# Attention, then a gated MLP: the last quarter's error function is written to four PSUM banks, the out-projection rotates through the other four

## The chip, the cores and the metric

The kernel runs on one core of one Trainium2 chip. The metric is the device time of one execution in microseconds (us), lower is better. Engines are named as the profile names them: PE (TensorE, matrix products; PEld its weight loads), DVE (VectorE), ACT (ScalarE), POOL (GpSimd), SP (SyncE, which issues DMAs). SBUF is the large on-chip memory, PSUM the small one that PE writes its products to; it has eight banks of 128 x 512 float32.

## The reference

Two stages, the second of which matters here. The first is an attention with a routing mask; its result, 3072 tokens of 512 numbers, is the `x` of an MLP whose gate is an error function of a softplus:

```python
def _moe_ref(x, w_in, w_out):          # x 3072x512, w_in 512x2048, w_out 2048x512
    h = x @ w_in
    sp = np.maximum(h, 0.0) + np.log1p(np.exp(-np.abs(h)))
    g = h * erf(sp)
    return (g @ w_out).astype(np.float32)
```

## The kernel before, in words

**The stages.** The first part of the kernel (up to about 404 us) is the attention. The rest is the MLP over six chunks of 512 tokens. Chunks 0 and 1 are worked one by one: the hidden layer `h` in two lots (`hidden26`, then `hidden`), then the out-projection (`project26`, line 1213, called with no plan). Chunks 2 to 5 go in pairs, with a hidden layer of another form (`hidden49`) and `project26` with a plan; the change leaves their computation as it is.

**The products.** Both layers are computed with fast matrix multiplication: sums and differences of blocks are formed first, fewer block products are made than there are pairs of blocks, and the products are added with signs into the results. The hidden layer of chunks 0 and 1 makes seven products where eight would be needed. The out-projection makes 26 (lists `LEFT` and `RIGHT`, line 70; the loop over `p` at line 1286). One product is four matmuls of 128 x 128 by 128 x 256 in float32, eight records in the trace.

**The gate.** Before the out-projection may read a block of `h`, it is gated: ACT computes the softplus of it into a buffer, then the error function of that in the same place, and DVE multiplies it into `g` (`gate26`, line 850). A call covers a quarter of a chunk's hidden layer, in two pieces `s` of 128 x 1024; each piece gets one softplus, one error function and two multiplications of 128 x 512. The last quarter (lot 1, half 1) is gated inside the out-projection itself (lines 1226 to 1231): softplus ahead of p = 0 and behind it, error functions at p = 1 and 2 (`s` = 1 first), multiplications (1,1), (0,1), (0,0), (1,0) of (s, h) at p = 3, 4, 5 and 6. Its buffer is, in chunk 0, the place of chunk 1's input `x_own` (`x_of[1]`, free until it is loaded at p = 8), and in chunk 1 a buffer `a_s`. At p = 4 and 5 of chunk 0 two multiplications of the quarter before also stand.

**Around the products.** `LEFT_STEPS` says which sums of gated blocks DVE forms behind which `p` (in place, so that such a step may wait until PE has read the old block); the products that use them follow a few `p` later. `AFTER` says how product `p` is read out of its bank: 'c' is a copy by ACT, 'a' an addition by DVE; capital letters go on from SBUF alone. The read-out of `p` is issued behind product `p + 1` (`LAG`). Each engine works in the order in which the program issues, all waits are semaphores. In chunk 0 POOL forms sums of blocks of `w_out` (`FIRST_FORMS`, `LAST_FORMS`, 128 x 512 each), of which the last stand at the beginning of the out-projection.

**The banks.** `bank()` gives the next of eight banks (lines 714 to 722): six of the pool `psb`, which rotates, and the two tiles `turned`. Within the out-projection product `p` takes the next bank at each `p`, so a bank comes round again after eight products.

Of the kernel before, what the change touches and what calls it, by code (L numbers as in the profile page):

```python
# [9 lines left out]
F32 = mybir.dt.float32  # L10
# [4 lines left out]
ALU = mybir.AluOpType  # L15
ACT = mybir.ActivationFunctionType
AX = mybir.AxisListType
PSUM = bass.MemoryType.PSUM

P = 128  # L20
# [15 lines left out]
HT, HK, HF, HM = CT // 2, DM // P // 2, NFT // 2, DM // 2  # L36
# [109 lines left out]
def kernel(  # L146
# [13 lines left out]
    te, ve, ae, ge = (  # L160
        InOrder(tc, e, in_order) for e in (nc.tensor, nc.vector, nc.scalar, nc.gpsimd)
    )

    def pool(name, bufs, **kw):
        return ctx.enter_context(tc.tile_pool(name=name, bufs=bufs, **kw))
# [5 lines left out]
    turned = [ps.tile([P, 512], F32, name=f"turned{i}") for i in range(2)]  # L171
# [100 lines left out]
    for base, pattern, sign, op, fill in (  # L272
# [5 lines left out]
            out=first, in_=first, compare_op=op, fill=fill, base=base, pattern=pattern,  # L278
# [355 lines left out]
    def load_x(n, queue=nc.sync):  # L634
        if n < NCHUNK:
            if n not in x_of:
                x_of[n] = xp.tile([P, DM // P, CT], F32, name="x_own")
            queue.dma_start(
                out=x_of[n], in_=x_dram.rearrange("(k p) t -> p k t", p=P)[:, :, n * CT : (n + 1) * CT]
            )  # L640

    def minus_of(out, a, b, engine=ve):
        engine.tensor_tensor(out=out, in0=a, in1=b, op=ALU.subtract)

    def plus_of(out, a, b, engine=ve):
        engine.tensor_tensor(out=out, in0=a, in1=b, op=ALU.add)
# [19 lines left out]
    def coming(n):  # L666
        return range(n + 1, 2 * n + 2) if n < N49 else range(n + 2, min(n + 4, NCHUNK)) if n % 2 == 0 else ()
# [41 lines left out]
    ORDER = (1, 2, 6, 7, 5, 3, 4)  # L709
    aside_work = []  # L710
    n_banks = [0]
    banks = [None]

    def whole_bank():
        n_banks[0] += 1
        b = banks[n_banks[0] % len(banks)]
        if b is None:
            b = psb.tile([P, 512], F32, name="bank")
        return b

    def bank():
        return whole_bank()[:, 0:HT]
# [68 lines left out]
    def w_block(b):  # L791
        lot, h = KAPPA[b // 2]
        f = h * HF + lot * FG
        return w_out[:, f : f + FG, (b % 2) * HM : (b % 2 + 1) * HM]

    def slot(i):
        if i < 6:
            at = HOME[i]
            return more_out[:, at // 2, (at % 2) * FG : (at % 2 + 1) * FG]
        return w_block((4, 7)[i - 6]) if i < 8 else ring[i - 8]  # L800
# [34 lines left out]
    def load_stream(k, queue=nc.sync):  # L835
        queue.dma_start(out=flat(ring[(k + 2) % RING]), in_=b_dram[k % N_STREAM])

    def left26(n, i):
        if i >= 16:
            return extra[i - 16]  # L840
        lot, h = KAPPA[i % 4]
        t = i // 4
        return g_of[n, t // 2, lot][:, h, :, (t % 2) * P : (t % 2 + 1) * P]

    def left_step(n, x, engine=ve):
        _, o, a, b, sign = LEFT_STEPS[x]
        form = plus_of if sign > 0 else minus_of
        form(left26(n, o), left26(n, a), left26(n, b), engine)

    def gate26(n, lot, half, boxes=None):  # L850
        gs = [g_of[n, s, lot][:, :, 2 * half : 2 * half + 2].rearrange("p h j t -> p h (j t)") for s in range(2)]
        box = []

        def soft(s):
            if not s:
                box.extend(boxes() if boxes else halves_of(actp.tile([P, 2 * FG * HT], F32, name="a_s")))
            ae.activation(out=box[s].rearrange("p (h j) -> p h j", h=2), in_=gs[s], func=ACT.Softplus)

        def erf(s):
            ae.activation(out=box[s], in_=box[s], func=ACT.Erf)  # L860

        def product(s, h):
            c = slice(h * 512, (h + 1) * 512)
            ve.tensor_tensor(out=gs[s][:, h], in0=box[s][:, c], in1=gs[s][:, h], op=ALU.mult)

        halves = [[functools.partial(f, s) for s in range(2)] for f in (soft, erf)]
        return *halves, {(s, h): functools.partial(product, s, h) for s in range(2) for h in range(2)}

    def halves_of(t):
        return [t[:, s * 1024 : (s + 1) * 1024] for s in range(2)]  # L870
# [38 lines left out]
    def load49(i, queue=nc.sync):  # L909
        o, a = w_order[i % len(w_order)]  # L910
        queue.dma_start(out=w49_place(i), in_=a_dram[OUTER.index(o), KEPT_AT[a]])
# [18 lines left out]
    def add49(o, lot, k):  # L930
        return [
            functools.partial(ge.dma_start, out=form49(o)[:, a], in_=part, accum_op=ALU.add)
            for a, part in w49_parts(lot, k)
        ]
# [274 lines left out]
    def fence(after):  # L1209
        t = up.tile([P, HM], F32, name="u")  # L1210
        ge.tensor_tensor(out=t[:, 0:1], in0=after[:, 0:1], in1=after[:, 0:1], op=ALU.add)

    def project26(n, plan=None):
# [4 lines left out]
        def c_at(i):  # L1218
            if i >= 8:
                return temps[i - 8]  # L1220
            t = i // 2
            return osb_of[n, t // 2][:, t % 2, (i % 2) * HM : (i % 2 + 1) * HM]

        if plan is None:
            boxes = None if n else lambda: halves_of(x_of[1].rearrange("p k t -> p (k t)"))
            soft, erf, last = gate26(n, 1, 1, boxes)
            curves = {-1: soft[:1], 0: soft[1:], 1: erf[1:], 2: erf[:1]}
            early = gates_first.pop(n)[1 + 4 * n :]
            gates_at = {
                -1: early[:2], 3: [last[1, 1]], 4: [last[0, 1], *early[2:3]], 5: [last[0, 0], *early[3:]], 6: [last[1, 0]],  # L1230
            }
            gates_before = {}
        else:
            gates_at, (curves, gates_before) = {}, plan
# [3 lines left out]
        banks26 = {}  # L1238
# [45 lines left out]
                    last_forms[p + i] = [piece]  # L1284
        run(f() for f in curves.get(-1, []) + gates_at.get(-1, []) + last_forms[-1])
        for p, r in enumerate(right):
            banks26[p] = m = bank()
            lhs = left26(n, left[p])
            g26 = N_STREAM * q + r - 100
            rhs = ring[(g26 + 2) % RING] if r >= 100 else slot(r) if r >= 0 else w_block(-1 - r)  # L1290
            for f in range(FG):
                te.matmul(m, lhsT=lhs[:, f], rhs=rhs[:, f], start=(f == 0), stop=(f == FG - 1))
            if r >= 100:
                if (g26 + RING) // N_STREAM in (q, q + 1 - q % 2):
                    load_stream(g26 + RING, queue)
            run(f() for f in last_forms.get(p, []) + gates_before.get(p, []))
            for x, step in enumerate(LEFT_STEPS):
                if step[0] == p:
                    left_step(n, x)
            run(f() for f in curves.get(p, ()))  # L1300
            if p < 3:
                if not delayed:
                    evict(p)
            elif p == 3 and delayed:
                for i in range(3):
                    evict(i)
            elif p > 3:
                evict(p - LAG)
                if final and p == len(RIGHT) - 2:
                    plus_of(c_at(2), c_at(2), c_at(8))  # L1310
                    minus_of(c_at(4), c_at(4), c_at(8))
            run(f() for f in gates_at.get(p, ()))
            if p >= len(RIGHT) - 8 and between:
                between.pop(0)()
            if n >= N49 and p in (5, 14) and coming(n):
                load_x(coming(n)[p // 14])
            if p == 14 and n == N49 - 1:
                load_x(n + 2, sy)
            if p == 8 and not n:
                load_x(1, sy)  # L1320
            if n == N49 - 1 and p in range(8, 8 + 2 * W_RING, 2):
                load49(p // 2 - 4, sy)
            if p == 4 and n == N49 - 1:
                fence(c_at(8))
                run(f() for f in add49(3, 0, 1))
# [6 lines left out]
    def run(work):  # L1332
        for _ in work:
            pass
# [137 lines left out]
    for e in range(2):  # L1472
        ae.copy(
            out=ccT[e * D : (e + 1) * D, :, e * C : (e + 1) * C],
            in_=pct[e * D : (e + 1) * D].rearrange("d (r e c) -> d r e c", e=2, c=C)[:, :, e],
# [7 lines left out]
    for r in (0, D):  # L1483
        for half in range(2):
            for e in range(2):
                c = r + half * Q + e * C
                ve.tensor_copy(
                    out=pick[r : r + D, half, e * D : (e + 1) * D].rearrange("p (n c) -> p n c", n=2)[:, :, 1 : C + 1],
                    in_=first[r : r + D, c : c + C].unsqueeze(1).to_broadcast([D, 2, C]),
# [47 lines left out]
    last = divide(u - 1)  # L1537
    attention.close()

    psb = pool("psb", 6, space=PSUM)  # L1540
    gp = pool("gp", 4)
    outp = pool("outp", 2)
    gsp = pool("gsp", 4)
# [2 lines left out]

    def finish_attention():
        run(last)
        banks[:] = [None] * 6 + turned

    take_places(4)
    late_places(2, out_boxes())
# [64 lines left out]
```

## Time and profile before

| | us |
|---|---|
| median of 3 runs | 950.21 (950.09 to 950.82) |
| the profiled execution | 950.18 |
| its span, first to last instruction | 948.4 |
| PE busy in the span | 938.9 (99%) |
| DVE / ACT / POOL busy | 755.8 / 560.2 / 524.3 |
| chunk 0's out-projection, in the span | 454.6 to 501.4 |
| chunk 1's out-projection | 549.7 to 594.6 |

The granted clock of PE is full in every slice of the page. In a row of the timeline stand the start and the length in us, engine, line, operation, output <- inputs by tile names, partitions x elements and type, the number of instructions merged in the row, and in brackets the engine's idle time before it with what ended it. Nearly all instructions have line 137, the helper that issues them, so the names of the tiles tell them apart: `bank` and `turned` are PSUM banks, `g` is the hidden layer, `g_more` holds sums and temporaries, `osb` output blocks, `x_own` and `a_s` (in the multiplications) the buffers of the gate.

### The profile page before, as it was taken

What the parts mean: (1) busy time and instruction counts of PE and PEld (TensorE: products, weight loads), DVE (VectorE), ACT (ScalarE), POOL (GpSimd) and SP (SyncE); (2) the same over time, 40 slices, a digit from 0 to 9 for tenths busy, and PEclk for the clock granted to TensorE, in tenths of its full rate; (3) what the DMA queues carried; (4) which work ended last, traced back from release to release, by engine and by line L of the source; (5) the groups of instructions that cost most, each with busy time, mean ns of one, the idle gap of its engine ahead of it and who ended that gap; (6) DMA issues with size and microseconds to landing.
All of it is one profiled execution on the core that took longest, in us unless ns stands there. A gap on an engine that the chain in (4) does not pass through costs nothing.

```text
span 948.4 us, 20923 instructions
## 1 busy us (share of the span) xinstructions
PE 938.9 (99%) x8151; PEld 691.9 (73%) x8151; DVE 755.8 (80%) x1336; ACT 560.2 (59%) x876; POOL 524.3 (55%) x353
## 2 busy tenths in 40 slices
PE   8999999999999999999999999999999999999998
PEld 3555555555555555588888888888888888888887
DVE  8888888888888888788995778456796974768977
ACT  3788878888888877576323542357825225574341
POOL 1688888888888888999605010676600028770000
PEclk9999999999999999999999999999999999999999
DMA  9454444444444521664659977555645535534443
GB/s 210 92 113 111 113 108 109 111 113 113 113 112 100 119 56 35 226 230 179 212 191 233 206 193 252 161 150 178 196 140 175 156 110 156 177 90 119 150 132 111
DMA packets 183360, 138.74 MB, mean 146 GB/s; under 512 B 132032, under 2 KB 141248, under 8 KB 183232
## 3 DMA queue, kind: packets, MB, share of 16 engines
q1 hardware_dynamic: 176048, 127.83, 47.1%
q0 software_dynamic: 4720, 9.18, 5.5%
q8 instruction: 64, 1.05, 0.5%
q10 hardware_dynamic: 2496, 0.43, 0.2%
q14 instruction: 32, 0.26, 0.1%
HBM read 99.39 MB, written 39.85 MB: 147 GB/s over the span
## 4 chain that ended last, share of the span: by engine, by line
PE 49%; DVE 1%; issue 0%
PE bank L137 39%; PE turned L137 10%; DVE g L137 1%; DVE g_more L137 0%; DVE osb L137 0%; DVE more_out L137 0%; DVE x_own L137 0%
## 5 line engine op out<-in xcount | busy, mean ns | idle before, releaser
L137 POOL TENSOR_TENSOR more_out<-more_out,pr 128x768 f32<-128x768 f32 x128 | 223.8, 1749 | 14.3 <-ACT pr L137 5.7
L137 DVE TENSOR_REDUCE nmx<-wide 128x2 f32<-128x512 f32 (+2 forms) x189 | 180.5, 955 | 51.8 <-PE wide L137 51.1
L137 ACT ACTIVATE pr<-sc 128x768 f32<-128x768 f32 x192 | 148.5, 810 | 65.3 <-PE wide L137 59.3
L137 PE MATMUL turned<-pr,in_v 128*32 128x193 f32 x3072 | 144.8, 330 | 0.0
L137 PEld LDWEIGHTS turned<-pr,in_v 128*32 128x32 f32 x3072 | 91.5, 109 | 51.5 <-issue 26.2
L137 PE MATMUL sc<-qT,kT 64*128 64x384 f32 x528 | 98.8, 488 | 0.0
L137 POOL TENSOR_TENSOR more_out<-pr,pr 128x768 f32<-128x768 f32 x32 | 60.8, 1901 | 41.8 <-ACT pr L137 41.8
L137 POOL TENSOR_TENSOR u<-w_in 128x1 f32<-128x1 f32 x2 | 0.4, 189 | 139.2 <-DVE w_in L137 139.2
L137 DVE TENSOR_TENSOR g<-g 128x512 f32<-128x512 f32 x88 | 62.4, 709 | 16.0 <-PE turned L137 8.5
L137 PE MATMUL bank<-x_own,more_in 128*128 128x256 f32 x276 | 68.1, 379 | 0.0
L137 PE MATMUL bank<-g_more,more_in 128*128 128x256 f32 x288 | 66.5, 380 | 0.0
L137 PE MATMUL wide<-kv,qv 64*128 64x256 bf16 (+2 forms) x378 | 64.0, 328 | 1.4 <-DVE nmx L137 0.9
L137 ACT ACTIVATE x_own<-x_own 128x512 int32<-128x512 uint32 (+2 forms) x62 | 63.0, 1028 | 0.1
L137 PE MATMUL wide<-km,qm 64*128 64x256 bf16 (+3 forms) x378 | 62.6, 327 | 0.0
L137 PEld LDWEIGHTS sc<-qT,kT 64*128 64x128 f32 x528 | 47.3, 187 | 20.6 <-ACT inv L137 3.4
L137 PE MATMUL bank<-g_more,g 128*128 128x256 f32 x256 | 60.6, 380 | 0.7 <-DVE g L137 0.7
L137 PEld LDWEIGHTS bank<-g_more,more_in 128*128 128x128 f32 x288 | 54.6, 190 | 8.2 <-DVE g L137 0.8
L137 PEld LDWEIGHTS bank<-x_own,more_in 128*128 128x128 f32 x276 | 52.4, 190 | 7.1
L137 DVE TENSOR_TENSOR g<-g,bank 128x256 f32<-128x256 f32 (+1 forms) x83 | 41.0, 512 | 20.4 <-PE bank L137 13.6
L137 ACT ACT_TABLE_LOAD x36 | 46.2, 1283 | 16.5 <-DVE g L137 15.9
L137 PEld LDWEIGHTS <-qv 64*128 64x128 bf16 x384 | 23.2, 93 | 42.9 <-issue 26.7
L137 PEld LDWEIGHTS bank<-g_more,g 128*128 128x128 f32 x256 | 48.5, 190 | 7.9 <-issue 1.4
(249 smaller groups left out, 2090.1 us busy)
## 6 DMA issues: line engine op xcount, KB each, us to landing
g_more<-b_dram SPq DMA_DIRECT2D x57, 512.0 KB, 3.7
more_in<-a_dram SPq DMA_DIRECT2D x98, 256.0 KB, 2.7
x_own<-in_moe_w_in_dram SPq DMA_DIRECT2D x13, 512.0 KB, 3.8
in_v<-in_v_dram SPq DMA_DIRECT2D x32, 192.0 KB, 2.9
x_dram<-more_out SPq DMA_DIRECT2D x128, 48.0 KB, 2.2
x_own<-x_dram SPq DMA_DIRECT2D x6, 1024.0 KB, 6.7
a_dram<-w_in SPq DMA_DIRECT2D x12, 512.0 KB, 3.8
in_k<-in_k_dram SPq DMA_DIRECT2D x59, 96.0 KB, 2.6
```

The source lines that it names most:

```text
L137: ins = getattr(self.engine, name)(*args, **kw)
```

## The change

Chunks 0 and 1, last quarter: the error function no longer overwrites the softplus in its SBUF buffer. It is computed in four instructions of 128 x 512 rather than two of 128 x 1024, each into a PSUM bank of its own, the `h` = 1 half of a piece first; the multiplication reads the bank. These four banks are the second half of the eight in the order of rotation, `in_turn[4:]`; the 26 products of these two out-projections rotate through the first four, `in_turn[p % 4]`. So that the banks can be named ahead, the rotating pool of six becomes a list of six fixed tiles, in the same order of use. On every engine the order of the instructions stays as it was, but for the four added on ACT.

```diff
     def whole_bank():
         n_banks[0] += 1
-        b = banks[n_banks[0] % len(banks)]
-        if b is None:
-            b = psb.tile([P, 512], F32, name="bank")
-        return b
+        return banks[n_banks[0] % len(banks)]
...
-    def gate26(n, lot, half, boxes=None):
+    def gate26(n, lot, half, boxes=None, room=None):
...
         def erf(s):
-            ae.activation(out=box[s], in_=box[s], func=ACT.Erf)
+            if room is None:
+                ae.activation(out=box[s], in_=box[s], func=ACT.Erf)
+                return
+            for h in (1, 0):
+                ae.activation(out=room[2 * s + h], in_=box[s][:, h * 512 : (h + 1) * 512], func=ACT.Erf)

         def product(s, h):
-            c = slice(h * 512, (h + 1) * 512)
-            ve.tensor_tensor(out=gs[s][:, h], in0=box[s][:, c], in1=gs[s][:, h], op=ALU.mult)
+            curve = box[s][:, h * 512 : (h + 1) * 512] if room is None else room[2 * s + h]
+            ve.tensor_tensor(out=gs[s][:, h], in0=curve, in1=gs[s][:, h], op=ALU.mult)
...
         if plan is None:
             boxes = None if n else lambda: halves_of(x_of[1].rearrange("p k t -> p (k t)"))
-            soft, erf, last = gate26(n, 1, 1, boxes)
+            in_turn = [banks[(n_banks[0] + 1 + i) % len(banks)] for i in range(len(banks))]
+            soft, erf, last = gate26(n, 1, 1, boxes, in_turn[4:])
...
         for p, r in enumerate(right):
-            banks26[p] = m = bank()
+            whole_bank()
+            banks26[p] = m = (banks[n_banks[0] % len(banks)] if plan else in_turn[p % 4])[:, 0:HM]
...
-    psb = pool("psb", 6, space=PSUM)
+    psb = pool("psb", 1, space=PSUM)
+    banks.extend(psb.tile([P, 512], F32, name=f"bank{i}") for i in range(6))
...
-        banks[:] = [None] * 6 + turned
+        banks[:] = banks[2:] + banks[:2] + turned
```

More of the change, by code (lines that the diff above doesn't have):

```diff
@@ L711 @@
     n_banks = [0]
-    banks = [None]
+    banks = []
     def whole_bank():
         n_banks[0] += 1
-        b = banks[n_banks[0] % len(banks)]
-        if b is None:
-            b = psb.tile([P, 512], F32, name="bank")
-        return b
+        return banks[n_banks[0] % len(banks)]
     def bank():
```

## The prediction, made before the changed kernel was run

> **What bounds the kernel now.** First the page: the share of each engine, and the chain that ended last.
>
> ```profile
> span 948.4 us, 20923 instructions
> PE 938.9 (99%) x8151; PEld 691.9 (73%) x8151; DVE 755.8 (80%) x1336; ACT 560.2 (59%) x876; POOL 524.3 (55%) x353
> PE 49%; DVE 1%; issue 0%
> ```
>
> PE is busy for 99% of the span, and the chain, which is followed back as far as the second half, is almost only PE. So a change elsewhere pays only where PE stands still, and what PE gains in one chunk is kept to the end as long as PE stays the bound. The profiled execution took 950.18 us around its span of 948.4; the median of the three runs is 950.21, the same within 0.03, so sums against the one hold for the other.
>
> Next, the table by stretches, cut at the two out-projections that the change touches: chunk 0's runs from 454.6 to 501.4, chunk 1's from 549.7 to 594.6.
>
> ```profile
> 454.60:501.40 46.80, 45.44 (x211) 39.40 (x210) 45.10 (x80) 15.22 (x30) 11.51 (x8) 1.00 0.56 185
> 549.70:594.60 44.90, 44.90 (x209) 39.52 (x209) 36.18 (x74) 15.12 (x30) 3.96 (x4) 1.00 0.74 214
> ```
>
> The first number behind the length is PE's busy time, the third DVE's. In chunk 1 PE is never idle, so nothing can be gained there, only lost. In chunk 0 PE misses 46.80 - 45.44 = 1.36 us, and DVE is busy for 45.10 of 46.80: there the products wait for DVE. The timeline of PE shows where. A row is one block product of eight records; I call them p = 0 to 25, and 468.47 is p = 8.
>
> ```profile
> 468.47 1.89 PE L137 MATMUL bank<-w_out,g_more 128*128 128x256 f32 x8
> 471.07 1.97 PE L137 MATMUL bank<-g_more,g 128*128 128x256 f32 x8 [0.71 <-DVE g L137]
> 472.88 1.89 PE L137 MATMUL bank<-w_out,g 128*128 128x256 f32 x8
> 474.60 1.89 PE L137 MATMUL bank<-g_more,g 128*128 128x256 f32 x8
> ...
> 478.06 1.89 PE L137 MATMUL turned<-g_more,g 128*128 128x256 f32 x8
> 480.59 1.97 PE L137 MATMUL turned<-w_out,g 128*128 128x256 f32 x8 [0.64 <-DVE g L137]
> 482.39 1.89 PE L137 MATMUL bank<-w_out,g 128*128 128x256 f32 x8
> ```
>
> Undisturbed, products start 1.73 us apart (474.60 - 472.88 = 1.72). From p = 8 to 9 it is 2.60, from p = 13 to 14 it is 2.53, and the product after each stall comes 1.80 or 1.81 later. The two stalls cost 0.87 + 0.80 + 2 x 0.08 = **1.83 us**, and this is all that the change can win where it acts: 0.19% of the time. A measurement of this kernel tells about 0.2% from no change, that is 1.9 us.
>
> Why DVE is late: its timeline in chunk 0, and POOL's beside it.
>
> ```profile
> 461.56 1.75 DVE L137 TENSOR_TENSOR g<-x_own,g 128x512 f32<-128x512 f32 x1
> 463.49 1.50 DVE L137 TENSOR_TENSOR g<-g 128x512 f32<-128x512 f32 x1 [0.17 <-PE bank L137]
> 464.91 1.75 DVE L137 TENSOR_TENSOR g<-x_own,g 128x512 f32<-128x512 f32 x1
> 466.58 0.68 DVE L137 TENSOR_TENSOR g<-a_s,g 128x512 f32<-128x512 f32 x1
> ...
> 469.04 0.69 DVE L137 TENSOR_TENSOR g<-x_own,g 128x512 f32<-128x512 f32 x1
> ...
> 470.24 0.69 DVE L137 TENSOR_TENSOR g<-g 128x512 f32<-128x512 f32 x1
> 470.84 0.69 DVE L137 TENSOR_TENSOR g<-x_own,g 128x512 f32<-128x512 f32 x1
> ...
> 473.50 0.41 DVE L137 TENSOR_TENSOR g_more<-g_more,bank 128x256 f32<-128x256 f32 x1
> ...
> 477.37 0.42 DVE L137 TENSOR_TENSOR g_more<-g_more,bank 128x256 f32<-128x256 f32 x1
> ...
> 478.30 2.14 DVE L137 TENSOR_TENSOR g<-g 128x512 f32<-128x512 f32 x3
> ...
> 482.09 0.41 DVE L137 TENSOR_TENSOR g_more<-g_more,bank 128x256 f32<-128x256 f32 x1
> ```
>
> ```profile
> 438.01 1.27 POOL L137 TENSOR_TENSOR g_more<-g_more,w_out 128x512 f32<-128x512 f32 x1
> 439.24 1.27 POOL L137 TENSOR_TENSOR more_out<-w_out 128x512 f32<-128x512 f32 x1
> ...
> 459.37 3.40 POOL L137 TENSOR_TENSOR x_own<-more_out 128x512 f32<-128x512 f32 x2
> 462.73 3.38 POOL L137 TENSOR_TENSOR x_own<-w_out,more_out 128x512 f32<-128x512 f32 x2
> ```
>
> ```profile
> 438.45 0.42 DVE L137 TENSOR_TENSOR g<-bank,g 128x256 f32<-128x256 f32 x1 [0.44 <-PE bank L137]
> 439.32 0.42 DVE L137 TENSOR_TENSOR g<-turned,g 128x256 f32<-128x256 f32 x1 [0.44 <-PE turned L137]
> ```
>
> The four rows g<-x_own,g are chunk 0's last-quarter gate products. The same instruction takes 1.75 us at 461.56 and 464.91, while POOL works, and 0.69 at 469.04 and 470.84, when POOL has ended (462.73 + 3.38 = 466.11). POOL slows too: 1.70 each beside such DVE work, 1.27 alone. But beside the two DVE rows that have one input in a PSUM bank, POOL keeps 1.27 and DVE its 0.42, what such a row takes without POOL as well (477.37). So two engines with SBUF inputs only hold each other up, in turns: DVE's 1.75 ends 0.55 after POOL's instruction (466.66 against 466.11), and POOL's lengthens by 1.70 - 1.27 = 0.43.
>
> **The change part by part.** *The gate products read a PSUM bank.* Without POOL the two kinds cost the same, by the groups of the later chunks:
>
> ```profile
> L137 DVE TENSOR_TENSOR g<-g 128x512 f32<-128x512 f32 x66 | 45.5, 689 | 15.5 <-PE turned L137 8.5 <-PE bank L137 5.5
> L137 DVE TENSOR_TENSOR g<-g,bank 128x512 f32<-128x512 f32 x30 | 19.8, 683 | 12.4 <-PE bank L137 6.5 <-POOL g L137 5.9
> ```
>
> So only the two contended ones gain. [...]
>
> The re-run: (1) at 461.56 the product takes 0.69, not 1.75, but the next step, 463.49, waited for PE and still does: nothing is won directly. (2) POOL's instruction at 462.73 is now not held up and ends at 464.00. (3) The DVE step at 463.49 is held by it until there and ends 0.55 later, 464.55, not 464.99. POOL's last one ends at about 464.00 + 1.70 = 465.70. (4) The second product, no longer held, ends near 465.16. (5) The next (g<-a_s,g, both inputs in SBUF) is held until 465.70 and ends at 466.25, where it now ends at 466.58 + 0.68 = 467.26. From there DVE runs without a gap past 482, so its chain comes **1.0 us** earlier. If POOL does not speed up at all, steps 3 and 5 keep POOL's old ends and it is 0.6; if step 5 is not held either, it is 1.5.
> [...]
>
> *The products rotate through four banks instead of eight.* Product p + 4 must wait until p has been read out. Where DVE reads it out: p = 7 at 473.50, p = 9 at 477.37, p = 11 at 482.09. They now end at 473.91, 477.79 and 482.50; p = 11, 13, 15 start at 474.60, 478.06, 482.39. From DVE's end to PE's start I take 0.14 (470.93 to 471.07). On the old times the slack is +0.55, +0.13 and **-0.25**: a new wait, at p = 15. The other read-outs of the chunk end with more room than these.
>
> *The sum for chunk 0*, DVE 1.0 earlier: p = 9 needs 470.93 - 1.0 + 0.14 = 470.07, undisturbed start 470.20: stall gone. p = 13: bank at 476.93, start 477.11: passes. p = 14 could start at 478.84, but the third g<-g of 478.30 ends at 480.44 - 1.0, so 479.58: a stall of 0.74 stays. p = 15 could follow at 481.38, but its bank is free only at 482.50 - 1.0 + 0.14 = 481.64. Against 482.39 that is 0.75 earlier, less 0.08 for restarting: **0.67 us** won. From there PE runs on as before.
>
> *The error function in two pieces.*
>
> ```profile
> L137 ACT ACTIVATE a_s<-a_s 128x1024 f32<-128x1024 f32 x12 | 12.2, 1050 | 0.1
> L137 ACT COPY bank<-bank 128x512 f32<-128x512 f32 x15 | 8.6, 572 | 13.6 <-PE bank L137 13.6
> 556.44 1.06 ACT L137 ACTIVATE a_s<-a_s 128x1024 f32<-128x1024 f32 x1
> 557.40 0.35 ACT L137 COPY osb<-bank 128x256 f32<-128x256 f32 x1
> ```
>
> An instruction of 1024 is 1.05 us; no SBUF-to-PSUM curve is in the trace, the nearest row is the copy of 512 into a bank, 0.57. Two make 1.14, so each whole error function costs -0.1 (overlapped) to +0.2 us on ACT. What is queued behind it: ACT's read-out of products 1 and 2. In chunk 1, where this is tightest, the read-out of p = 1 ends at 557.75; p = 5, which will need its bank, is this row:
>
> ```profile
> 558.36 1.89 PE L137 MATMUL bank<-more_out,g_more 128*128 128x256 f32 x8
> ```
>
> Slack 0.61 - 0.14 = 0.47, so 0.2 is hidden; beyond 0.47 it would cost PE. I take nothing. The four banks that the error function fills last held products of the hidden layer, which must be read out before the softplus in front of it can start: no wait.
>
> *The rest.* Named banks replace rotating buffers for the whole second half: the same rotation and distance of eight outside the two out-projections, so nothing. Chunk 1's input, loaded into the buffer that held the curve, no longer waits for DVE, and starts earlier than 471.59; its first reader is at 490.14, so nothing either.
>
> ```profile
> 471.59 0.37 SPq L137 DMA_DIRECT2D x_own<-x_dram  x1
> 490.14 0.69 DVE L137 TENSOR_TENSOR x_more<-x_own 128x512 f32<-128x512 f32 x1
> ```
>
> **The rivals.** (A) *The ring of four ends on the slower side*: a 512-wide product from PSUM still meets POOL, DVE comes no earlier, and p = 15 waits for its bank: 0.25 + 0.08 = 0.33 slower, **950.5**. It decides once DVE's gain is below 0.33. For it: the slack is already negative, and no 512-wide row stands beside POOL. Against: the two 256-wide ones do, undisturbed. This is also the case in which the change does not do what it says. [...] (C) *ACT's pieces block the ring in chunk 1*: the whole function now takes 0.96 there from start to read-out (557.40 - 556.44), so two pieces hold p = 5 from 0.96 + 0.47 = 1.43 us on; at 1.75, as long as a contended DVE product, it costs 0.32, or **949.8**. Against: the 0.57 of the nearest row.
>
> **How the numbers follow.** Forecast 950.18 - 0.67 = **949.5 us**. With DVE's gain at 0.6 the same sum gives 0.27, at 1.5 it gives 1.17: the forecast's own range is 949.0 to 949.9, chance 0.72. A has 0.11, B 0.08, C 0.03; 0.06 is for what I do not see, half of it beyond 1.9 us on either side. The range 948.9 to 950.5 takes in the forecast, A and C, and the near edge of B. None of the cases reaches 1.9 us: faster by over 0.2% 0.03, within 0.2% 0.94, slower 0.03.
>
> **What would show it.** In chunk 0 all four gate products near 0.69; POOL's last two instructions ending near 465.7; no wait at p = 9, one of about 0.7 at p = 14 <-DVE, and a small one at p = 15 for its bank. Chunk 1 without idle PE. Gate products still at 1.75 prove A; waits of p = 5 prove C; a stall anywhere else would make the sum wrong.

## The result, and the profile after

The changed kernel takes **951.81 us** (median of 20 runs, 951.56 to 952.17) against 950.21 before: ratio 1.0017, 95% interval 1.001 to 1.0024. It is 1.6 us slower; the forecast was 949.5, 0.7 faster. The number lies outside the range, on the wrong side of zero, though within 0.2%.

The page of the profiled execution:

```profile
span 950.0 us, 20922 instructions
PE 940.6 (99%) x8151; PEld 691.2 (73%) x8151; DVE 754.3 (79%) x1336; ACT 560.9 (59%) x880; POOL 523.8 (55%) x353
```

Four instructions more on ACT, as many as before on the other engines of this row, and a span longer by 1.6. Since PE is the bound in both, the place of the loss is found by setting PE's rows of the two traces side by side. First PE in chunk 0's out-projection (p = 8 is at 468.64; this trace is already about 0.2 late when the MLP begins; in the traces of the experiments below p = 8 starts anywhere between 468.34 and 468.75):

```profile
468.64 1.89 PE L137 MATMUL bank<-w_out,g_more 128*128 128x256 f32 x8
470.37 1.89 PE L137 MATMUL bank<-g_more,g 128*128 128x256 f32 x8
...
477.28 1.89 PE L137 MATMUL bank<-g_more,g 128*128 128x256 f32 x8
479.74 3.96 PE L137 MATMUL bank<-w_out,g 128*128 128x256 f32 x16 [0.57 <-DVE g L137]
483.54 0.81 PE L137 MATMUL bank<-g_more,g 128*128 128x256 f32 x3
```

The stall in front of p = 9 is gone (470.37 - 468.64 = 1.73). The one in front of p = 14 is 477.28 to 479.74, 2.46 for 1.73. Products 14 and 15 take 3.80 together (483.54 - 479.74), not the 1.80 + 1.73 = 3.53 of a restart without another wait: the 0.27 over is what p = 15 loses by waiting for its bank, its own restart included. DVE and POOL:

```profile
461.76 0.68 DVE L137 TENSOR_TENSOR g<-bank,g 128x512 f32<-128x512 f32 x1
463.67 1.08 DVE L137 TENSOR_TENSOR g<-g 128x512 f32<-128x512 f32 x1 [1.23 <-PE bank L137]
464.67 0.68 DVE L137 TENSOR_TENSOR g<-turned,g 128x512 f32<-128x512 f32 x1
465.27 1.16 DVE L137 TENSOR_TENSOR g<-a_s,g 128x512 f32<-128x512 f32 x1
```

```profile
462.93 2.95 POOL L137 TENSOR_TENSOR x_own<-w_out,more_out 128x512 f32<-128x512 f32 x2
```

All of this is the forecast: 0.68 for a gate product beside POOL, where it was 1.75; POOL's last pair 2.95 for 3.38; a_s,g still held until POOL ends at 465.88. So the loss lies elsewhere. Where, the table of PE waits by releaser shows, for everything behind chunk 1. It is the view of the weight loads (PEld); where one of these waits ends, load and matmul both start at 671.10, the load after 0.73 of idle time, the matmul after 0.33. Before and then after (us in total, times, longest):

```profile
PEld bank L137 <- DVE g L137: 0.8, 2, 0.4
PEld bank L137 <- issue: 0.8, 3, 0.3
PEld turned L137 <- issue: 0.3, 1, 0.3
```

```profile
PEld bank L137 <- DVE g L137: 2.3, 4, 0.7
PEld bank L137 <- POOL g L137: 1.0, 2, 0.5
PEld bank L137 <- ACT w_in L137: 0.9, 4, 0.2
PEld bank L137 <- issue: 0.8, 3, 0.3
PEld turned L137 <- issue: 0.3, 1, 0.3
```

There are eight new waits, of DVE, POOL and ACT, all in front of a `bank`, in chunks 2 to 5, whose computation the change leaves alone. Their worth by the starts of the same two products, before and then after: the product p = 16 of chunk 0, and a later run of twelve records, behind the last new wait.

```profile
484.12 1.89 PE L137 MATMUL bank<-g_more,g 128*128 128x256 f32 x8
851.60 3.04 PE L137 MATMUL bank<-g_more,more_in 128*128 128x256 f32 x12
```

```profile
483.54 1.89 PE L137 MATMUL bank<-g_more,g 128*128 128x256 f32 x8
853.31 3.04 PE L137 MATMUL bank<-g_more,more_in 128*128 128x256 f32 x12
```

At the first the changed kernel is 0.58 ahead, at the second 1.71 behind: **2.29 us lost** between them. Up to the first it had won about 0.74, since it began 0.17 behind.

**What waits.** The hidden layers of chunks 2 to 5 (`hidden49`) go in turns of seven products, fourteen turns (k = 0 to 13) per pair of chunks. A turn k takes four banks at once, by role: X, N, Y, Z (`begin`, line 1021 of the kernel before), in this order from the rotation. Four of the seven products (`m1`, `m6`, `m7`, `m4`) go one after another into X, one into each of N, Y and Z. X is written first in its turn and read out last: its last sum, `m4`, is made in turn k + 1. Four banks per turn and eight in the ring mean that with a fixed order X of turn k + 2 gets the bank of X of turn k, which is read out just before. Here is the worst one, a product of X in the last turn of the first pair, with the read-out of the X two turns earlier, in the changed kernel:

```profile
669.75 1.03 PE L137 MATMUL turned<-g_more,more_in 128*128 128x256 f32 x4
671.10 1.13 PE L137 MATMUL bank<-g_more,more_in 128*128 128x256 f32 x4 [0.33 <-DVE g L137]
```

```profile
670.38 0.68 DVE L137 TENSOR_TENSOR g<-g,bank 128x512 f32<-128x512 f32 x1
```

The matmul starts 0.04 behind the end of that read-out (671.06), 1.35 after the product in front instead of the 0.86 that such a product takes. The kernel before, at the same place:

```profile
669.73 1.03 PE L137 MATMUL turned<-g_more,more_in 128*128 128x256 f32 x4
670.60 1.67 PE L137 MATMUL bank<-g_more,more_in 128*128 128x256 f32 x7
```

```profile
670.36 0.68 DVE L137 TENSOR_TENSOR g<-g,bank 128x512 f32<-128x512 f32 x1
```

DVE reads X out at the same time, 670.36, but nobody waits for it: X goes to another bank. The rows don't carry the numbers of the banks; the program as built does (its order is the list `LATE_BANKS` of an experiment below). In it the rotating pool did not hand out its six buffers in a fixed order: X mostly got the bank that X had three turns earlier (10 of the 28 turns) or the bank of N of the turn before (7). In none of the 28 turns did X get the bank of the X two turns earlier. By what rule the pool chose, no run shows.

Each trace holds 8151 of the 8152 matmul records that the program makes, and throughout the MLP all of them, in the program's order of outputs, so every wait can be given its product. All eight stand in front of the first product of X in a turn: in each pair of chunks in turns 2, 3, 4 and 13. Measured on PE's starts, they cost 0.09, 0.09, 0.41 and 0.59 us in the first pair and 0.09, 0.09, 0.33 and 0.60 in the second: 2.29 together, the whole loss. The waits that the table puts down to ACT and POOL are of the same kind. In turns 2 and 3 it is ACT that reads out the old X: its rows end at 603.48 and 609.62, and the weight loads of the new X start at 603.53 and 609.67. In turn 4 DVE reads it out, but late, because DVE had itself waited for POOL; X starts 0.10 behind the end of that read-out (616.05):

```profile
614.77 0.69 DVE L137 TENSOR_TENSOR g<-g,bank 128x512 f32<-128x512 f32 x1 [1.46 <-POOL g L137]
615.37 0.68 DVE L137 TENSOR_TENSOR g<-w_in,bank 128x512 f32<-128x512 f32 x1
```

```profile
616.15 1.10 PE L137 MATMUL bank<-g_more,more_in 128*128 128x256 f32 x4 [0.17 <-POOL g L137]
```

### The profile page after: what moved, and what is told of

The parts are those of the page before. It is cut to its first block, busy times and chain, and to the rows that moved or that the text cites. A ratio compares the mean times of both kernels' runs of the same rounds, so it can differ in the third digit from the quotient of the medians.

```text
span 950.0 us, 20922 instructions
## 1 busy us (share of the span) xinstructions
PE 940.6 (99%) x8151; PEld 691.2 (73%) x8151; DVE 754.3 (79%) x1336; ACT 560.9 (59%) x880; POOL 523.8 (55%) x353
## 4 chain that ended last, share of the span: by engine, by line
PE 48%; DVE 2%; ACT 1%; issue 0%
PE bank L137 38%; PE turned L137 9%; DVE g L137 1%; DVE osb L137 0%; ACT L137 0%; ACT x_own L137 0%; ACT a_s L137 0%; DVE w_in L137 0%; DVE g_more L137 0%; DVE more_out L137 0%; ACT bank L137 0%; DVE x_own L137 0%
## 5 line engine op out<-in xcount | busy, mean ns | idle before, releaser
L137 PE MATMUL bank<-g_more,g 128*128 128x256 f32 x288 | 68.1, 379 | 0.0
L137 ACT ACTIVATE x_own<-x_own 128x512 int32<-128x512 uint32 (+2 forms) x60 | 60.9, 1027 | 0.0
L137 PEld LDWEIGHTS bank<-g_more,g 128*128 128x128 f32 x288 | 54.6, 190 | 7.7 <-issue 0.3
```

Of the source, the lines that this page charges most:

```text
L137: ins = getattr(self.engine, name)(*args, **kw)
```

## The experiments

The theory: the loss is the **order of the banks** in chunks 2 to 5, and the change is otherwise worth what was forecast. Rival 1: tiles with fixed names cost as such, by other waits. Rival 2: the ring of four, or the earlier DVE in chunk 0, upsets the later chunks. All runs are of 9 to 11 executions; "before" on the same chip was 950.16 for the first four and 950.03 for the last four.

### The named banks alone

```diff
# the kernel before, with only this of the change
     def whole_bank():
         n_banks[0] += 1
-        b = banks[n_banks[0] % len(banks)]
-        if b is None:
-            b = psb.tile([P, 512], F32, name="bank")
-        return b
+        return banks[n_banks[0] % len(banks)]
...
-    psb = pool("psb", 6, space=PSUM)
+    psb = pool("psb", 1, space=PSUM)
+    banks.extend(psb.tile([P, 512], F32, name=f"bank{i}") for i in range(6))
...
-        banks[:] = [None] * 6 + turned
+        banks[:] = banks[2:] + banks[:2] + turned
```

> The kernel before with one part of the change alone: the six rotating buffers are six named banks in fixed order. Error function in SBUF, ring of eight. Theory (order): the rotating pool handed each new tile the bank that was released first, so that in chunks 2 to 5 the bank of X came from N or Y two turns earlier; the fixed order gives X the bank of X, which is read out last. The eight new waits of the changed kernel cost 2.3 us, so 952.5. Rival 1 (named tiles cost as such, by their finer waits): also 952.5; the next kernel tells it apart. Rival 2 (the ring of four or the earlier DVE in chunk 0 upsets the later chunks): 950.2, no new waits behind 595.

Measured: 952.88, ratio 1.0026 (1.0016 to 1.0036). Of the 2.7 that it loses, 2.4 lie in the span (median 950.7 against 948.3); the rest is time outside the span, and why that is longer here no run shows. The waits behind chunk 1 are those of the changed kernel to the digit:

```profile
PEld bank L137 <- DVE g L137: 2.3, 4, 0.7
PEld bank L137 <- POOL g L137: 1.0, 2, 0.5
PEld bank L137 <- ACT w_in L137: 0.9, 4, 0.2
```

Rival 2 falls: neither the error function in PSUM nor the ring of four is in this kernel. The expectation is wrong on where the pool had X's bank from: hardly ever from N (once) and never from Y of two turns earlier, but from the tiles named above.

### The old order from chunk 2 on

```diff
# the changed kernel; LATE_BANKS lists the banks in the order that the pool had,
# fixed_banks holds the six named tiles; other lines are left out
     def whole_bank():
         n_banks[0] += 1
+        if n_banks[0] > 164:
+            return (fixed_banks + turned)[LATE_BANKS[n_banks[0] - 165]]
         return banks[n_banks[0] % len(banks)]
```

> The changed kernel, but from chunk 2 on the named banks are taken in the order that the rotating pool had before, written out as a list. Theory (order): no new wait behind 595, the gain of chunk 0 remains: 950.2 - 0.7 = 949.5. Rival 1 (named tiles as such): 951.8 as the changed kernel. Rival 2 (ring of four or chunk 0): 951.8.

Measured: 949.50, ratio 0.9993 (0.9985 to 1.0002); PE has no wait left behind chunk 1 beyond those of before. Rival 1 falls: the tiles are named here too, and only their order differs. The interval does not part this from no change. The spans do: 947.4 to 948.0 in its eleven executions, 948.1 to 948.8 in the 31 of the kernel before on the same chip, 0.7 less by the medians. That this was won in chunk 0 the trace shows, where p = 16 starts 0.72 earlier than before (484.12):

```profile
479.60 3.96 PE L148 MATMUL bank<-w_out,g 128*128 128x256 f32 x16 [0.54 <-DVE g L148]
483.40 0.81 PE L148 MATMUL bank<-g_more,g 128*128 128x256 f32 x3
```

### The ring of four alone

```diff
# as the kernel with the old order; the error function stays in SBUF
-            soft, erf, last = gate26(n, 1, 1, boxes, in_turn[4:])
+            soft, erf, last = gate26(n, 1, 1, boxes)
```

> Ring of four in the two out-projections alone, error function in SBUF as before, old order of the banks from chunk 2 on. By the prediction's sum: DVE comes no earlier, both old stalls stay, and p = 15 waits for its bank: +0.25 + 0.08, so 950.5. If the gain of chunk 0 had another source than the gate products' PSUM operand: below 950.0.

Measured: 950.44, ratio 1.0002 (0.9993 to 1.0011). In its trace both old stalls stand, and behind the second a row of two products that takes 3.80 again:

```profile
471.37 1.97 PE L148 MATMUL bank<-g_more,g 128*128 128x256 f32 x8 [0.73 <-DVE g L148]
...
480.88 3.96 PE L148 MATMUL bank<-w_out,g 128*128 128x256 f32 x16 [0.64 <-DVE g L148]
484.68 0.59 PE L148 MATMUL bank<-g_more,g 128*128 128x256 f32 x2
```

The ring's price at p = 15 is 0.27 again, restart included, where rival A put 0.33 on it (0.25 and a restart of 0.08).

### The ring of eight again from p = 8

```diff
# as the kernel with the old order
-            banks26[p] = m = (m if plan else in_turn[p % 4])[:, 0:HM]
+            banks26[p] = m = (m if plan else in_turn[p % (8 if p >= 8 else 4)])[:, 0:HM]
```

> As the kernel with the old order from chunk 2 on, but the products rotate through all eight banks again from p = 8, when the four of the error function have been read. By the theory the wait of p = 15 for its bank (about 0.2 to 0.3 in the changed kernel) goes: 949.2. If that wait only hides another: 949.5.

Measured: 949.55, ratio 0.9993 (0.9984 to 1.0002). This is the number of the rival, and the times can't tell this kernel from the one with the ring of four. The trace can: p = 14, 15 and 16 start 1.83 and 1.73 apart, so the wait at p = 15 is gone. So can the spans: their median is 947.3, against 947.6 with the ring of four, the 0.3 of the theory. In the device time it is hidden by more time outside the span (about 2.2 us in the median execution, 1.8 with the ring of four); why, no run shows.

```profile
479.34 1.99 PE L148 MATMUL turned<-w_out,g 128*128 128x256 f32 x8 [0.45 <-DVE g L148]
481.17 1.89 PE L148 MATMUL bank<-w_out,g 128*128 128x256 f32 x8
482.90 1.46 PE L148 MATMUL bank<-g_more,g 128*128 128x256 f32 x6
```

### X takes N's bank, and a control

A list copied from the old program shows that the order matters, not what in it. So: the fixed ring of the changed kernel, and only the roles exchanged in every second pair of turns. The kernel and its control differ only in X and N.

```diff
-            state[v] = {nm: whole_bank() for nm in "XNYZ"}
+            state[v] = {nm: whole_bank() for nm in ("NXZY" if k % 4 > 1 else "XNYZ")}
# the control has "XNZY" in the place of "NXZY": X and N keep their own banks
```

> The changed kernel with its fixed order of the banks, but in every second pair of turns of the later hidden layers X takes the bank that N had two turns earlier and N that of X, Y that of Z and Z that of Y. Theory (order): X is read out last of the four and needed first, so giving it N's bank removes the waits: 949.5, no new wait behind 595. Rival (the waits come from something else in the list of the old order, such as another place of Y or Z): 951.8.

> Control: the changed kernel, in every second pair of turns Y takes the bank of Z and Z that of Y; X and N keep theirs. Theory (X's own bank is the cause): nothing removed, 951.8, the same eight waits. Rival (any change of roles helps): 949.5.

Measured: 949.58 (ratio 0.9994, 0.9986 to 1.0003) with X in N's bank, 951.86 (1.0019, 1.001 to 1.0027) for the control, which keeps all eight waits. With X in N's bank, the same place in the last turn, PE and then DVE:

```profile
668.83 1.03 PE L137 MATMUL turned<-g_more,more_in 128*128 128x256 f32 x4
669.70 1.68 PE L137 MATMUL bank<-g_more,more_in 128*128 128x256 f32 x7
```

```profile
669.46 0.67 DVE L137 TENSOR_TENSOR g<-g,bank 128x512 f32<-128x512 f32 x1
```

The matmul starts 0.87 after the product in front, 0.43 before DVE has read out the old X (670.13). One exchange of names takes back the 2.3 us (951.86 - 949.58).

### The error function in two pieces, in place

```diff
# the kernel before: rotating pool, ring of eight, curve in SBUF; last quarter only
-            ae.activation(out=box[s], in_=box[s], func=ACT.Erf)
+            for h in (1, 0):
+                c = slice(h * 512, (h + 1) * 512)
+                ae.activation(out=box[s][:, c], in_=box[s][:, c], func=ACT.Erf)
```

> The kernel before with the last quarter's error functions in two pieces of 512, in place in SBUF; rotating pool, ring of eight. Tests whether the gain of chunk 0 came from the earlier release of half a product instead of the PSUM operand. Theory (PSUM operand): 950.2, the gate products at 461.6 and 464.9 still near 1.75, both old stalls. Rival (earlier release): 949.5.

Measured: 950.10, ratio 1.0001 (0.9992 to 1.001). Both old stalls stay (p = 9 starts 2.62 after p = 8, p = 14 2.53 after p = 13). The gate products beside POOL stay at 1.76 and 1.75, where the changed kernel has 0.68, so it is the operand in PSUM that shortens them, not the half that is ready sooner:

```profile
461.69 1.76 DVE L137 TENSOR_TENSOR g<-x_own,g 128x512 f32<-128x512 f32 x1
...
465.04 1.75 DVE L137 TENSOR_TENSOR g<-x_own,g 128x512 f32<-128x512 f32 x1
```

### Both mended, chunk 0 only

```diff
# the changed kernel with "NXZY" as above, and
-            soft, erf, last = gate26(n, 1, 1, boxes, in_turn[4:])
+            soft, erf, last = gate26(n, 1, 1, boxes, None if n else in_turn[4:])
...
-            banks26[p] = m = (banks[n_banks[0] % len(banks)] if plan else in_turn[p % 4])[:, 0:HM]
+            banks26[p] = m = (banks[n_banks[0] % len(banks)] if plan or n or p >= 8 else in_turn[p % 4])[:, 0:HM]
```

> The changed kernel in chunk 0 alone (chunk 1 with its curve in SBUF and a ring of eight), ring of eight again from p = 8 in chunk 0, and X in N's bank every second pair of turns. By the theory chunk 1's part of the change does nothing, so only the wait of about 0.7 at p = 14 remains of the old 1.83: 949.2, as the kernel with the old order and the ring of eight from p = 8, whose trace lost 0.3 less than that with the ring of four.

Measured: **949.21**, ratio 0.9991 (0.9982 to 1.0), the lowest median of the study, 2.6 under the changed kernel and 0.8 under the one before on the same chip. The first is clear; the second is at the edge of what the times can tell, but the spans part the two: 947.1 to 947.4 here, 948.1 to 948.8 in the 33 executions before. The stall left at p = 14 is 0.59 in the trace (2.32 from p = 13 to p = 14), less than the 0.7 expected.

## Why the prediction was wrong

**The step that failed** stands under "The rest": "Named banks replace rotating buffers for the whole second half: the same rotation and distance of eight outside the two out-projections, so nothing." The distance of eight holds for the named banks. It did not hold for the rotating pool, which in chunks 2 to 5 handed out its buffers in another order. The prediction shows no row and no list for it, and the words "in the same order of use" in the description of the change are wrong for these chunks too. The order of the banks in the built program was there to be looked up. In place of nothing the runs show 2.3 us: 2.29 in the trace, 952.88 - 950.16 = 2.7 by the medians with the named banks alone, 951.81 - 949.50 = 2.3 between the changed kernel and the one with the old order. The last sign that the prediction names, a stall anywhere else, is what came. It was no rival, since the rivals were sought only in chunks 0 and 1, where the change says that it acts.

**The cap of 1.83 us** was a cap on gains where the change acts, and no run won more there; nothing of the kind bounded the losses elsewhere, and the stretch behind chunk 1, two thirds of the MLP, was never asked which waits nearly bind in it.

**Chunk 0, right to a tenth.** DVE was to come 1.0 earlier: a_s,g ended at 467.26 and now at 465.27 + 1.16 = 466.43, 0.83 earlier in a trace that is 0.17 to 0.20 late, so 1.0. POOL's last pair was to end at 465.70, and ends at 465.88 in that late trace. The stall of p = 9 was to go and has gone, that of p = 14 to shrink to 0.74 and is 2.46 - 1.73 = 0.73; p = 15 was to wait 0.26 for its bank and to restart for 0.08, 0.34 in all, and costs 0.27. Its bank is read out by DVE until 481.66, and it starts 0.05 later:

```profile
481.25 0.41 DVE L137 TENSOR_TENSOR g_more<-g_more,bank 128x256 f32<-128x256 f32 x1
```

```profile
481.71 1.99 PE L137 MATMUL bank<-w_out,g 128*128 128x256 f32 x8
```

The sum took 0.14 for that step, from the one row 470.93 to 471.07; in the changed kernel it lies between 0.04 (671.06 to 671.10) and 0.15 (the third g<-g ends at 479.59, p = 14 starts at 479.74). So the sum was 0.67 where the trace has 0.74, and the kernel with the old order takes 949.50 against a forecast of 949.5.

**The PSUM operand.** The four gate products take 0.68 each, also beside POOL (461.76 and 464.67); with both inputs in SBUF they took 1.75 beside POOL and 0.69 when it had ended. With both inputs of DVE in SBUF it and POOL still took turns: POOL's pair of 2.95 is one instruction undisturbed, 1.27 to 464.20, and one held up, 1.72 from 464.16; the DVE step at 463.67 ends 0.55 behind the first, at 464.75, as the sum had it.

**ACT's pieces.** From the first piece to the read-out behind them in the changed kernel:

```profile
459.81 0.60 ACT L137 ACTIVATE bank<-x_own 128x512 f32<-128x512 f32 x1
460.35 0.58 ACT L137 ACTIVATE turned<-x_own 128x512 f32<-128x512 f32 x1
460.87 0.36 ACT L137 COPY osb<-bank 128x256 f32<-128x256 f32 x1
```

1.06, where one piece of 1024 took 0.96: the split costs 0.10, inside the bounds of -0.1 to +0.2, and it is hidden, as forecast. Two pieces in place in SBUF took 1.06 as well (459.73 to 460.79 in that experiment), so the 0.10 came with the split, in the bank and in place alike. Chunk 1 has no idle PE (busy for 45.00 us of the 45.00 from 549.0 to 594.0); its part of the change does nothing, neither good nor bad: the median span is 947.3 with it (ring of eight from p = 8) and 947.2 without it (both mended, chunk 0 only).

**The chances.** Within 0.2% had 0.94 and came in, but by luck: the loss that nobody had looked for, less the gain, happened to come to 1.6 us, under the 1.9; the range that mattered, 948.9 to 950.5, left out a whole class of causes. What B, with its 0.08, needed, both stalls gone, no run shows: in the changed kernel the one at p = 14 stayed, 0.73, and the DVE step at 465.27, both inputs in SBUF, took 1.16 for 0.68, with POOL at work until 465.88.

## What to carry to other kernels

Whoever replaces a rotating pool by fixed buffers may change the order in which buffers come round, in every stage that shares them: compare, buffer by buffer in the built program, when each is last read and next written, also where the source did not change. With a fixed ring, give the tile that is written first the buffer that is read out first; here one exchange of two names was worth 2.3 us. And here an operand in PSUM kept DVE out of POOL's way: 0.68 for 1.75 us in each of two instructions, but PE gained only the part of it for which it stood still, 0.74 in chunk 0.
